# Issuing the load of the fifth weight chunk ahead of the fourth token tile's in the opening of a four-layer kernel

## The chip, the cores and the metric

The kernel runs on one core of one Trainium2 chip. The metric is the device time of one execution in microseconds (us), of which the profile's span, from the first to the last recorded instruction, is about 1.8 us less. TensorE is called PE, VectorE DVE, ScalarE ACT, GpSimd POOL; SyncE's sequencer, which issues all the loads, is SPq. Every timed run here is of the fast state, and the granted TensorE clock was 1.00 in every profile; two runs that were only looked at (e7, e8: one execution each) have no state, and only their traces are used.

## The reference, cut to what matters

Four layers over 2048 tokens of 1024 numbers (bf16), each on a layer norm and added to its input. The first and third are a linear attention, the second and fourth a gated bilinear block. Only the start of the first matters here.

```python
x = A_x
x = x + _A_ref(_layernorm(x, axis=-1), A_wqkv, A_wo)      # q, k, v = x @ wqkv; phi = exp/relu; ...
x = x + _B_ref(_layernorm(x, axis=-1), B_w_gate, B_w_up, B_w_down)
x = x + _A_ref(_layernorm(x, axis=-1), A_wqkv, A_wo)
x = x + _B_ref(_layernorm(x, axis=-1), B_w_gate, B_w_up, B_w_down)
```

## The kernel before

The tokens are cut into 16 tiles of 128 (token tile 0 is the first), the K weights into eight chunks of 128 rows (chunk 4 is the fifth). Each of these loads is 256 KB. The loads are issued from one queue in program order:

```python
    load_x(0)
    load_x(1)
    for k in range(0, 3):
        load_k(k, k + 1)
    load_x(2)
    load_k(3, 4)
    load_x(3)
    for k in range(4, 8):
        load_k(k, k + 1)
```

The first two token tiles are centred (their mean is subtracted) and turned (transposed) on PE. Then PE multiplies them by each weight chunk as it lands, two matmuls of 512 columns per tile and chunk (`k_part(t, a, b)` is tile t with chunks a to b-1). Tiles 2 and 3 are turned by DMA and follow when all eight chunks are there.

```python
            # ... tiles 0 and 1 with chunks 0 to 2, in between their transposes ...
            mean_by_halves(2, 2)
            centre_by_halves(2, 2)
            turn(XN[:, 2, :], 0, 2)            # DMA transpose of tile 2
            ln_stats(3)                        # DVE: statistics of tile 3 ...
            centre(3, stat[3][0][:, 0:1])
            turn(XN[:, 3, :], 0, 3)            # ... and its DMA transpose
            load_q()                           # the Q weights, two loads of 1 MB
            for t in range(4, NT):
                load_x(t)
            for t in range(3):
                ln_stats(t)                    # DVE: statistics of tiles 0 to 2
            for k in range(3, 6):
                for t in range(2):
                    k_part(t, k, k + 1)        # PE: chunks 3, 4, 5
            for t in range(2):
                k_part(t, 6, 8)                # PE: chunks 6 and 7 together; then phi on ACT
            k_part(2, 0, 8)
            k_part(3, 0, 8)
            # ... then the Q products of tiles 0 to 3, and so on; all that follows is unchanged
```

DVE takes its instructions in the order of the program: in the trace it begins the statistics of tile 3 at 9.54 us and those of tile 0 at 11.50. So `ln_stats(3)` stands ahead of the statistics of tile 0, which ACT's first exponential (`phi` of tile 0) needs. `phi` reads a tile's sums twice, for an exponential and for a maximum with 0. The sums stand in PSUM, the memory that PE writes, which has three places for them here; token tile 3 takes over tile 0's, and that is free only when ACT has read it.

Of the kernel before, what the change touches and what calls it, by code (L numbers as in the profile page):

```python
# [26 lines left out]
def kernel(  # L27
# [80 lines left out]
    def load(dst, src):  # L108
        nc.sync.dma_start(out=dst, in_=src)  # L109

    def load_x(t):
        load(X[:, t, :], x_view[:, t, :])

    def load_k(a, b):
        load(wkv[:, a:b, :], wqkv_v[:, a:b, D:2 * D])
# [22 lines left out]
    for k in range(0, 3):  # L138
        load_k(k, k + 1)
    load_x(2)  # L140
    load_k(3, 4)
    load_x(3)
    for k in range(4, 8):
        load_k(k, k + 1)


# [506 lines left out]
```

## Time and profile before

| | before |
|---|---|
| time, median of 3 | 1622.03 us (1621.81 to 1622.1) |
| span of the profile | 1620.1 us |
| PE busy | 99% |
| PE's waits for loads, whole kernel | one, ahead of chunk 4 |
| first matmul on chunk 4 | 10.24 us |
| first matmul of token tile 2 | 13.69 us |

The prediction below shows the lines on which this rests. One view more is needed: the issues of a narrow stretch, once around 4.0 us and once around 4.5 us. The last column is the time from issue to landing.

```profile
X<-in_A_x_dram SPq DMA_DIRECT2D x1, 256.0 KB, 5.5
...
W<-in_A_wqkv_dram SPq DMA_DIRECT2D x1, 256.0 KB, 5.7
```

Token tile 3, issued at 4.01, lands at 9.51; chunk 4, issued at 4.48, at 10.20. Both are well over 5 us under way, while the loads ahead of them land one by one: from token tile 2 on, one place in the row is 0.65 to 0.72 us. What an order of issue decides here is the order of landing. This is why exchanging two lines of the program could matter at all.

### The profile page before, as it was taken

The numbers are of one execution on the slowest core, as the hardware profiler recorded it, in microseconds if no ns is written. First come the engines' busy times: TensorE is split into PE (matmuls) and PEld (weight loads), VectorE is DVE, ScalarE is ACT, GpSimd is POOL, SyncE is SP. The second block draws the span as 40 slices with busy tenths as digits, with TensorE's granted clock in tenths as the row PEclk, the third lists the DMA queues.
The fourth block names the chain that finished last, engine by engine and source line by source line (L and its number), as shares of the span: only waits on it lengthen the run. The fifth ranks groups of instructions, "written<-read, shape, count | busy, mean of one in ns | idle before, by whom it ended". The sixth has DMA issues, their size and how long they took to land.

```text
span 1620.1 us, 18047 instructions
## 1 busy us (share of the span) xinstructions
PE 1607.5 (99%) x7710; PEld 734.5 (45%) x7861; DVE 616.6 (38%) x946; ACT 284.0 (18%) x384; POOL 54.5 (3%) x135
## 2 busy tenths in 40 slices
PE   9999999999999999999999999999999999999999
PEld 4444444444444444444444444444444444444444
DVE  6899853202311321243255798432123113211111
ACT  5522201101110110011045231011011101101110
POOL 2100000000000000010000000000000000000000
DMA  8224856512650552142420257655236306521400
GB/s 247 53 72 93 246 162 176 162 52 60 171 159 0 147 162 81 52 156 66 92 52 1 78 114 219 181 157 165 69 102 175 127 20 173 165 66 65 156 1 26
DMA packets 236719, 183.10 MB, mean 113 GB/s; under 512 B 102368, under 2 KB 217312, under 8 KB 236640
## 3 DMA queue, kind: packets, MB, share of 16 engines
q1 hardware_dynamic: 236640, 181.95, 39.0%
q8 instruction: 61, 1.00, 0.3%
q14 instruction: 18, 0.15, 0.0%
HBM read 153.09 MB, written 4.19 MB: 97 GB/s over the span
## 4 chain that ended last, share of the span: by engine, by line
PE 99%; issue 1%; DMA 0%; SPq 0%; DVE 0%
PE ps L196 50%; PE ps L538 48%; PE ps L565 1%; DMA W<-in_A_wqkv_dram 0%; PE kv L306 0%; SPq L109 0%; PE pm L328 0%; PE ps L328 0%; DVE X L546 0%
## 5 line engine op out<-in xcount | busy, mean ns | idle before, releaser
L538 PE MATMUL ps<-xT,R 128*128 128x512 bf16 x2382 | 525.9, 379 | 2.6
L538 PEld LDWEIGHTS <-R 128*128 128x128 bf16 x2432 | 238.0, 98 | 286.9
L542 DVE TENSOR_TENSOR R<-gs,ps 128x512 bf16<-128x512 f32 x224 | 153.9, 687 | 533.5 <-ACT gs L541 533.5
L196 PEld LDWEIGHTS <-R 128*128 128x128 bf16 x2248 | 220.0, 98 | 265.2
L541 ACT COPY gs<-ps 128x512 f32<-128x512 f32 x224 | 131.3, 586 | 1040.2 <-PE ps L538 1011.5
L538 PE MATMUL ps<-xT,W 128*128 128x512 bf16 x1130 | 250.4, 379 | 1.2
L196 PEld LDWEIGHTS <-xT 128*128 128x128 bf16 x1536 | 149.5, 98 | 181.4 <-issue 1.9
L196 PE MATMUL ps<-W,xT 128*128 128x512 bf16 x997 | 222.8, 379 | 1.9 <-issue 0.3
L538 PEld LDWEIGHTS <-W 128*128 128x128 bf16 x1152 | 112.7, 98 | 135.9
L196 PE MATMUL ps<-W,R 128*128 128x512 bf16 x733 | 170.1, 379 | 0.8
L546 DVE TENSOR_TENSOR X<-X,ps 128x1024 bf16<-128x1024 bf16 (+3 forms) x34 | 39.4, 1158 | 335.8 <-PE ps L196 282.8
L196 PE MATMUL ps<-R,R 128*128 128x512 bf16 x506 | 111.8, 379 | 0.4
L196 PE MATMUL ps<-PQ,R 128*128 128x512 bf16 x488 | 111.4, 379 | 0.5
L196 PE MATMUL ps<-R,xT 128*128 128x512 bf16 x502 | 110.3, 379 | 0.5
L201 ACT ACTIVATE e<-ps 128x1024 bf16<-128x1024 f32 x56 | 57.3, 1024 | 141.2 <-PE ps L196 86.0
L175 DVE BATCH_NORM_STATS2 st<-X 128x6 f32<-128x512 bf16 x128 | 81.7, 680 | 0.1
L179 POOL TENSOR_SCALAR ve<-mv 128x1 f32<-128x1 f32 x64 | 16.2, 254 | 1325.8 <-DVE mv L177 1325.8
L196 PE MATMUL ps<-GL,R 128*128 128x512 bf16 x240 | 57.8, 379 | 0.3
L196 PE MATMUL ps<-xT,R 128*128 128x512 bf16 x240 | 57.5, 379 | 0.2
L378 DVE TENSOR_TENSOR X<-X,ps 128x1024 bf16<-128x1024 bf16 x32 | 38.7, 1209 | 17.0 <-PE ps L196 17.0
L186 DVE TENSOR_SCALAR R<-X,mv,rstd 128x1024 bf16<-128x1024 bf16 x64 | 33.7, 542 | 27.3 <-POOL rstd L181 24.0
L205 DVE TENSOR_SCALAR e<-e 128x1024 bf16<-128x1024 bf16 x64 | 26.9, 421 | 38.1 <-ACT e L201 38.1
(73 smaller groups left out, 456.6 us busy)
## 6 DMA issues: line engine op xcount, KB each, us to landing
R<-in_B_w_gate_dram SPq DMA_DIRECT2D x38, 1024.0 KB, 5.4
R<-in_B_w_up_dram SPq DMA_DIRECT2D x38, 1024.0 KB, 7.6
W<-in_B_w_gate_dram SPq DMA_DIRECT2D x18, 1024.0 KB, 5.4
W<-in_B_w_up_dram SPq DMA_DIRECT2D x18, 1024.0 KB, 7.6
W<-in_A_wqkv_dram SPq DMA_DIRECT2D x10, 1024.0 KB, 6.2
W<-in_B_w_down_dram SPq DMA_DIRECT2D x6, 1024.0 KB, 11.2
X<-in_A_x_dram SPq DMA_DIRECT2D x16, 256.0 KB, 6.7
PQ<-in_B_w_down_dram SPq DMA_DIRECT2D x4, 1024.0 KB, 8.4
```

The costliest lines, as they stand in the source:

```text
L175: nc.vector.bn_stats(out=st[:, c, :], in_=X[:, t, c * NB:(c + 1) * NB])
L179: nc.gpsimd.tensor_scalar(out=ve[:], in0=mv[:, 1:2], scalar1=1e-5, scalar2=None, op0=ALU.add)
L186: nc.vector.tensor_scalar(out=dst, in0=X[:, t, :], scalar1=mv[:, 0:1], scalar2=rstd[:], op0=ALU.subtract, op1=ALU.mult)
L196: nc.tensor.matmul(out=ps[:, n, :], lhsT=lhsT, rhs=rhs[:, n * NB:(n + 1) * NB], start=start, stop=stop)
L201: nc.scalar.activation(out=e[:], in_=flat(ps), func=ACT.Exp, **sc)
L205: nc.vector.tensor_scalar(out=e[:], in0=e[:], scalar1=1.0, scalar2=EPS, op0=ALU.min, op1=ALU.add)
L378: nc.vector.tensor_tensor(out=X[:, t, :], in0=X[:, t, :], in1=flat(ps), op=ALU.add)
L538: nc.tensor.matmul(out=ps[:, n, :], lhsT=w[:, k, j * P:(j + 1) * P], rhs=xT[g % 2][:, k, :], start=(k == 0), stop=(k == KD - 1))
L541: nc.scalar.copy(out=gs[:], in_=ps[:, 0, :])
L542: nc.vector.tensor_tensor(out=hT[:, f, :], in0=gs[:], in1=ps[:, 1, :], op=ALU.mult)
L546: nc.vector.tensor_tensor(out=X[:, t, a:b], in0=X[:, t, a:b], in1=ps, op=ALU.add)
L565: nc.tensor.matmul(out=ps[:, 0, 0:b - a], lhsT=hT[:, f, tl * P:(tl + 1) * P], rhs=wd[f][:, a:b], start=(f == 0), stop=(f == KF - 1))
```

## The change

It is meant to have the chunk that PE waits for land one place earlier, at the cost of the token tile that is needed later. The whole diff:

```diff
     load_x(2)
-    load_k(3, 4)
+    for k in (3, 4):
+        load_k(k, k + 1)
     load_x(3)
-    for k in range(4, 8):
+    for k in range(5, 8):
         load_k(k, k + 1)
```

## The prediction

> **What bounds the kernel now.** I read the page first, then the chain of work that ended last, then the opening (the first 41 us) in the timeline, because the diff touches only the order of twelve loads there.
>
> The page's busy shares and the summary of the chain:
>
> ```profile
> PE 1607.5 (99%) x7710; PEld 734.5 (45%) x7861; DVE 616.6 (38%) x946; ACT 284.0 (18%) x384; POOL 54.5 (3%) x135
> ...
> PE 99%; issue 1%; DMA 0%; SPq 0%; DVE 0%
> ```
>
> TensorE (PE) is busy for 99% of 1620.1 us, and the chain is 99% PE. No other engine is above 38%. A change that adds and removes no instruction can only win time in which PE stands still. So the next question is where PE waits. The list of who waited for whom, PE's own, over the whole span, has four entries:
>
> ```profile
> PE ps L165 <- PEq L637: 0.8, 1, 0.8
> PE pt L403 <- DVE R L419: 0.7, 1, 0.7
> PE ps L196 <- issue: 0.3, 2, 0.2
> PE ps L196 <- DMA W<-in_A_wqkv_dram: 0.2, 1, 0.2
> ```
>
> Columns: total us, times, longest. The last one is the only wait for a load, and W is the tile into which the K weight chunks go. The chain of the opening says which chunk it is:
>
> ```profile
> 4.48 5.72 DMA W<-in_A_wqkv_dram
> 10.20 0.04 issue
> 10.24 2.10 PE ps L196 x9
> 12.35 0.05 issue
> 12.40 10.74 PE ps L196 x49
> ```
>
> Start, length, what. The transfer issued at 4.48 us lands at 10.20, and PE goes on at 10.24. The issues of the SyncE queue identify it:
>
> ```profile
> 3.06 0.43 SPq L109 DMA_DIRECT2D X<-in_A_x_dram  x1
> 3.53 0.43 SPq L109 DMA_DIRECT2D W<-in_A_wqkv_dram  x1
> 4.01 0.43 SPq L109 DMA_DIRECT2D X<-in_A_x_dram  x1
> 4.48 2.46 SPq L109 DMA_DIRECT2D W<-in_A_wqkv_dram  x4
> ```
>
> These are token tile 2 (the third), chunk 3 (the fourth), token tile 3 (the fourth), then chunks 4 to 7. So chunk 4, the one that the change moves, is exactly the one that PE waits for. That makes the change well aimed; what remains is how large the wait is and what comes right behind it. PE's own timeline around it:
>
> ```profile
> 6.80 3.22 PE L196 MATMUL ps<-W,xT 128*128 128x512 bf16 x14
> 10.24 10.95 PE L196 MATMUL ps<-W,xT 128*128 128x512 bf16 x49 [0.22 <-DMA W<-in_A_wqkv_dram]
> ```
>
> **What the Trainium skill says.**
> - "Perfetto Trace Analysis", section "Summary: the profiler window per engine type": a matmul's reported end is estimated, its start is observed. So I don't use the 0.22 us but starts: the last matmul of chunk 3 starts at 9.646, the first of chunk 4 at 10.241, 0.595 apart, where its neighbours are 0.216 apart. The true standstill is 0.595 - 0.216 = **0.38 us**.
> - "TensorE: Matmul & The Clock Gate", section "Back-to-back issue gap": 512 columns cost N/2.4 + 2.5, thus 215.8 ns, warm. The trace agrees (0.216, granted clock 1.00 in this stretch). The same section gives 131 ns as the sustained figure; the trace doesn't agree.
> - "DMA: Bandwidth & Descriptors", section "Queues, rings and completion order": descriptors of one queue are consumed in ring order, while completions need not be. Here they do come in order of issue, 0.6 to 0.7 us apart from token tile 2 on (below). So exchanging two issues should exchange two landings.
>
> **The change, part by part.** Nothing is added or removed: the comparison of instruction orders shows the same rows on PE, VectorE (DVE), ScalarE (ACT) and GpSimd, and on SyncE the fourth token tile and the fifth chunk have changed places. Both are 256 KB. From the trace's records of each transfer, landings before: token tile 2 8.18, chunk 3 8.84, token tile 3 9.51, chunk 4 10.20, chunk 5 10.87, chunk 6 11.53, chunk 7 12.25 us. After, by exchange: chunk 4 at 9.51, token tile 3 at 10.20, the rest unmoved.
>
> *PE's side.* Each chunk serves two token tiles with two matmuls each: 4 x 0.216 = 0.863 us. From a landing to PE's start is 0.04 us (10.199 to 10.241).
> - Chunk 4: PE is ready at 9.646 + 0.216 = 9.86, landing 9.51. No wait; start 9.86 instead of 10.24, 0.38 won.
> - Chunk 5: PE ready at 9.86 + 0.86 = 10.73, but landing + 0.04 = 10.91. A **new wait of 0.18 us**; start 10.91 instead of 11.10, 0.19 left.
> - Chunk 6: ready at 11.77, landed 11.53. No wait.
> - Chunk 7: the loop takes chunks 6 and 7 together for each token tile, so chunk 7 is wanted two matmuls later, at 11.77 + 0.43 = 12.20. Landing + 0.04 = 12.29. A **second new wait of 0.09 us**. Start 12.29 where it was 12.40.
>
> Thus the last chunk decides: its landing doesn't move, and before the change PE reached it only 0.15 us after it landed, of which 0.04 is needed anyway. The gain is 12.397 - 12.291 = **0.11 us**, of 0.38 us in sight. From 12.40 on PE runs in one piece, and the later waits are few and for its own helpers, so these 0.11 us should reach the end.
>
> *The side that pays.* Token tile 3 lands 0.69 us later. DVE starts its statistics at 9.54 today, straight after other work, 0.03 after the landing; after the change it must wait until about 10.23. Behind it in DVE's order stand the centring of tile 3 and the statistics of tiles 0 to 2, which the first exponential on ACT needs:
>
> ```profile
> ACT e L201 <- POOL rstd L181: 5.0, 1, 5.0
> ```
>
> So the whole string shifts by 0.69 us. What does PE notice?
> - Transpose of tile 3 lands at 14.76, later 15.45; its matmuls begin at about 17.04. Slack 1.6.
> - PSUM: the matmuls of tile 3 wait for ACT to have read tile 0's sums. ACT ends that at 16.14, later 16.83; wanted at 17.04 (12.29 + 6 x 0.216 + 16 x 0.216). **Slack 0.2**, 0.15 with a semaphore.
> - Q weights, issued behind the transposes: second half lands at 21.23, later 21.92; wanted at about 22.21. **Slack 0.29**.
> So both stay just hidden. Nothing to subtract.
>
> Sum: 1622.03 - 0.11 = 1621.9 us.
>
> **The rivals.**
> 1. *The whole wait goes*: 0.38 us, thus 1621.65. For it: chunk 4's wait is the only one that the views show. Against: the landings of chunks 5 and 7 are 0.24 and 0.15 us ahead of PE today and come by the same full queue. It would need all of them to come earlier, and the change gives them nothing.
> 2. *The late token tile makes a new stall*: if tile 3 slips by 0.9 us or more rather than 0.69, ACT frees PSUM too late or the Q weights come too late, and PE loses 0.1 to 0.5 us; the time would be 1622.0 to 1622.4. For it: slacks of only 0.2 to 0.3. Against: equal sizes, evenly spaced landings.
> 3. *Nothing to be seen*: the three runs of before differ by 0.29 us (1621.81 to 1622.1), more than the gain. If landings wander by 0.1 us between executions, the gain is between nought and 0.2 and drowns. This is what I expect of the end-to-end times, with the trace showing the steps.
>
> A loss or gain of 2% would be 32 us. All of PE's waits in the opening together are 1.7 us, so neither is within reach.
>
> **Range and chances.** Centre 1621.9. Downwards, rival 1 plus the scatter of before gives 1621.4; upwards, rival 2 gives 1622.4; 0.1 us more on each side for another day's scatter. Within 2%: 0.99.
>
> **What would show it.** In the changed kernel's profile: (a) chunk 4 lands near 9.5 and token tile 3 near 10.2; (b) PE's one wait for W, 0.22 us long by the view, gives way to two smaller ones, before chunk 5 (0.18 by starts, so hardly visible in the view because the modelled matmul ends cover 0.16 of any wait) and before chunk 7 (0.09, invisible there); (c) the matmul that first uses chunk 7 starts at about 12.29 instead of 12.40; (d) DVE idles about 0.65 us before the statistics of tile 3, and ACT's first exponential begins at about 14.7 instead of 14.02; (e) no new PE wait at 17.0 or 22.2. It would be wrong if landings do not follow the order of issue, if chunk 7 lands at another time than 12.25, or if (e) fails.

## The result, and the profile after

| | before | changed |
|---|---|---|
| median of 6 runs | 1622.07 us | 1621.88 us |
| lowest to highest | 1621.67 to 1622.96 | 1621.26 to 1622.7 |
| span of the profile | 1620.1 us | 1620.2 us |

The ratio is 0.9999, with a 95% interval from 0.9986 to 1.0011: the same. (A ratio is the mean time of one kernel's runs over that of the other's of the same rounds, so not quite the ratio of the medians.)

The span of the changed kernel is even 0.11 us longer, though its time is shorter. That asks for the trace. First a trap: the page of the changed kernel says

```profile
PE 1616.5 (100%) x7861; PEld 734.9 (45%) x7861; DVE 616.7 (38%) x946; ACT 283.8 (18%) x384; POOL 54.3 (3%) x135
```

PE seems 9 us busier than before. It isn't: before, the trace held 7710 matmul records for 7861 weight loads, so 151 were missing. For that reason the starts below are taken from the weight loads, one to each matmul and complete in both. (While PE runs without a gap, the weight load for the next matmul starts within 0.01 us of the matmul before it.)

The issues at 4.01 and 4.49 us of the changed kernel, in the same view as above:

```profile
W<-in_A_wqkv_dram SPq DMA_DIRECT2D x1, 256.0 KB, 5.7
...
X<-in_A_x_dram SPq DMA_DIRECT2D x1, 256.0 KB, 5.8
```

The two have changed places: chunk 4 landed at 9.68 (before 10.20), token tile 3 at 10.33 (before 9.51). The chain of the opening, changed kernel:

```profile
4.96 6.05 DMA W<-in_A_wqkv_dram
11.01 0.04 issue
11.06 11.97 PE ps L197 x54
```

The chain no longer ends at the transfer issued at 4.48 but at the next, issued at 4.96: chunk 5. PE now waits for that one. And it waits again behind it, which this view doesn't show. The timeline of the weight loads does, first before, then changed; of the idle time in brackets 0.12 us stands between any two loads:

```profile
8.57 1.18 PEld L196 LDWEIGHTS <-xT 128*128 128x128 bf16 x6
10.24 3.77 PEld L196 LDWEIGHTS <-xT 128*128 128x128 bf16 x18 [0.50 <-issue]
...
9.04 1.60 PEld L197 LDWEIGHTS <-xT 128*128 128x128 bf16 x8 [0.35 <-issue]
11.06 1.17 PEld L197 LDWEIGHTS <-xT 128*128 128x128 bf16 x6 [0.42 <-issue]
12.51 1.39 PEld L197 LDWEIGHTS <-xT 128*128 128x128 bf16 x7 [0.28 <-issue]
```

So PE waited 0.38 us ahead of chunk 4 before, and 0.30 us ahead of chunk 5 and 0.16 us ahead of chunk 7 in the changed kernel; in this execution also 0.24 us ahead of chunk 3, which the change leaves alone. The first matmul of token tile 2 began at 13.80, 0.11 later than before, and every later instruction of PE kept this offset to the end (1617.26 for the last weight load, against 1617.15). So the whole difference of the two spans was made in the first 14 us. But chunk 7 landed at 12.47 in this trace and at 12.25 in the other, though the loads ahead of it are the same eleven. Is that the change's doing, or does it wander?

DVE paid as expected. Its line for the statistics of tile 3, in DVE's timeline:

```profile
10.36 1.29 DVE L176 BATCH_NORM_STATS2 st<-X 128x6 f32<-128x512 bf16 x2 [1.26 <-DMA X<-in_A_x_dram]
```

In brackets stands the idle time before it and what ended it: the landing of the late token tile. Before, it began at 9.54 straight after other work. ACT's first exponential followed at 14.84 instead of 14.02. PE noticed nothing of it: ACT had read tile 0's sums at 16.96, and PE wanted their place at 17.25.

### The profile page after: what moved, and what is told of

Its sections match the earlier page's. It is cut to its first block, busy times and chain, and to the rows that moved or that the text cites. A ratio compares the mean times of both kernels' runs of the same rounds, so it can differ in the third digit from the quotient of the medians.

```text
span 1620.2 us, 18198 instructions
## 1 busy us (share of the span) xinstructions
PE 1616.5 (100%) x7861; PEld 734.9 (45%) x7861; DVE 616.7 (38%) x946; ACT 283.8 (18%) x384; POOL 54.3 (3%) x135
## 4 chain that ended last, share of the span: by engine, by line
PE 99%; DMA 0%; SPq 0%; issue 0%; DVE 0%
PE ps L197 50%; PE ps L539 48%; PE ps L566 1%; DMA W<-in_A_wqkv_dram 0%; PE kv L307 0%; SPq L109 0%; PE pm L329 0%; PE ps L329 0%; DVE X L547 0%
```

## The experiments

The theory: in the changed kernel the landing of the last chunks sets when PE gets to token tile 2, in the kernel before that of chunk 4, and these two are worth almost the same. The rivals: the change costs a fixed 0.1 us; the late token tile does not matter; or it does, and costs as much as was won.

### e1 and e2: both kernels once more

No edit. Five timed runs and one more trace of each.

> The kernel before, unchanged, against itself: how far times and landings wander. Theory (the landing of the last weight chunk sets the start of token tile 2 in the changed kernel, and almost does so before): landings move by up to 0.2 us from one execution to the next, PE waits only ahead of chunk 4 (0.3 to 0.5 us by starts), and the start of token tile 2's K matmuls follows the landing of chunk 4, about 3.5 us after it. Rival (landings are steady, and the 0.1 us by which the changed kernel's profiled run came out longer is a cost of the change): landings within 0.05 us of 10.20 for chunk 4 and 12.25 for chunk 7. Ratio of times 1.000 either way, scatter of the single runs some 0.5 us.

> The changed kernel, unchanged, once more. Theory: PE waits ahead of chunk 5 and chunk 7, and token tile 2's K matmuls start 1.34 us after the landing of chunk 7 (0.04 and six matmuls of 0.216 us), whatever that landing is; 13.6 us if it is 12.25, 13.8 if it is 12.47. Rival (the change costs a fixed 0.1 us): token tile 2 starts at 13.8 again although chunk 7 lands at 12.25. Ratio of times within 0.0005 of 1.

Times: before 1621.94 us (median of 5) against 1621.76 of the nine runs of the same kernel beside it, ratio 1.0 (0.9987 to 1.0012); changed 1621.99, ratio 1.0001 (0.9988 to 1.0013). So the times can't tell 0.1 us: the same kernel differs from itself by 0.18 in the median. In the trace of e1 PE waited 0.23 us ahead of chunk 4, less than the 0.3 to 0.5 expected, and 0.16 ahead of chunk 1, which was not expected.

The traces can. PE's timeline of the changed kernel:

```profile
6.66 5.21 PE L197 MATMUL ps<-W,xT 128*128 128x512 bf16 x23
12.05 9.23 PE L197 MATMUL ps<-W,xT 128*128 128x512 bf16 x42 [0.18 <-DMA W<-in_A_wqkv_dram]
```

Here PE's wait for a load has moved from chunk 4 to chunk 7, which landed at 12.01. (The view says 0.18 because a matmul record is missing; by starts it is 0.13, after 0.05 ahead of chunk 5.) The chain of the same trace jumps from that landing straight to token tile 2 and beyond:

```profile
6.16 5.86 DMA W<-in_A_wqkv_dram
12.01 0.04 issue
12.05 10.74 PE ps L197 x49
```

The start of token tile 2 in all traces of the two kernels, a third look at the changed one (e8, below) included:

| trace | chunk 4 lands | chunk 5 | chunk 7 | token tile 2 starts |
|---|---|---|---|---|
| before, first | 10.20 | 10.87 | 12.25 | 13.69 |
| before, e1 | 10.28 | 10.95 | 12.30 | 13.78 |
| changed, first | 9.68 | 11.01 | 12.47 | 13.80 |
| changed, e2 | 9.25 | 10.59 | 12.01 | 13.35 |
| changed, e8 | 9.88 | 11.24 | 12.50 | 13.87 |

Before: 3.49 and 3.50 us after chunk 4. Changed: 1.34 and 1.34 us after chunk 7, and in e8 2.63 us after chunk 5. These are the prediction's steps: 0.04 us and sixteen, six or twelve matmuls of 0.216. The fixed cost falls: the start of token tile 2 follows the landings of its own trace (13.35 with chunk 7 at 12.01, where that rival asked for 13.8 again), and the working below leaves nothing over for it. Landings wander by up to 0.65 us in the changed kernel alone (chunk 5), where the rival of e1 asked for 0.05; e1 alone, off by 0.08 and 0.05, would hardly have decided that.

To take the luck out, I ran the prediction's own recursion (PE takes a chunk when it is done with the one before it or 0.042 us after its landing, whichever is later; 0.2158 us a matmul) on each trace's landings and its start of chunk 3, once in either order, chunk 4 taking the eighth or ninth place of landing:

| trace | tile 2 measured | order before | order changed | difference |
|---|---|---|---|---|
| before, first | 13.694 | 13.694 | 13.586 | 0.11 |
| before, e1 | 13.775 | 13.777 | 13.639 | 0.14 |
| changed, first | 13.802 | 13.826 | 13.803 | 0.02 |
| changed, e2 | 13.347 | 13.393 | 13.349 | 0.04 |
| changed, e8 | 13.868 | 14.052 | 13.869 | 0.18 |

For the kernel that ran, it meets the measured start within 0.002 us each time. The other column is an estimate, since one execution has one order only. By it the change is worth 0.02 to 0.18 us, 0.10 in the mean.

One thing came unlooked for. In e2 the 0.35 us by which the opening was ahead of the first trace of before held until 972 us and were gone after it. PE's timeline there shows sixteen small matmuls (32*32, each with its own `tile_position` in the program), of which these two lines hold four:

```profile
971.93 0.39 PE L329 MATMUL ps<-PQ,KVb 32*32 32x512 bf16 x2
972.29 0.39 PE L329 MATMUL pm<-PQ,KVb 32*32 32x512 bf16 x2
```

In the traces without this gap all sixteen start within 0.05 us; here the ninth starts 0.36 us after the eighth, and it waits for no semaphore. e8 and e10 come back to it.

### e3 and e4: token tile 3 later still

e3 loads it after all the chunks, e4 after chunk 5.

```diff
     load_x(2)
-    load_k(3, 4)
+    for k in range(3, 8):        # e4: range(3, 6)
+        load_k(k, k + 1)
     load_x(3)
-    for k in range(4, 8):        # e4: range(6, 8)
-        load_k(k, k + 1)
```

> Token tile 3 is loaded after all eight chunks, so that chunk 7 lands a whole place earlier (about 11.55) and token tile 3 at about 12.25. Theory: PE's waits for chunks vanish and token tile 2 starts at about 13.3 (0.38 earlier than before), but the statistics of tile 3 stand ahead of those of tile 0 on DVE, so ACT's first exponential slips by 2.7 us to about 16.8, ACT frees tile 0's sums at about 18.9, and PE stands still some 2.1 us before token tile 3's matmuls: the kernel is 1.8 us slower than before (1.3 to 2.2), ratio 1.0011. Rival (the landing of token tile 3 has slack and does not matter): no stall, 0.4 us faster.

> Token tile 3 one place later still than in the changed kernel, behind chunk 5; it lands at about 10.9 to 11.0. Theory: PE waits only ahead of chunk 7 (0.25 us), token tile 2 starts 1.34 us after that landing as in the changed kernel, so nothing more is won; but ACT frees tile 0's sums 1.36 us later than before, at 17.5, where PE wants them at 17.0: a stall of about 0.5 us before token tile 3, the kernel 0.4 us slower than before (0.2 to 0.7). Rival (the slack of 0.2 us was reckoned too small): no stall, 0.1 us faster than before.

e3: 1623.54 us against 1621.76 before, 1.78 more; ratio 1.0013 (1.0001 to 1.0026; one of its five runs, 1625.63, lies apart from the other four, 1623.26 to 1623.94). PE's waits in e3:

```profile
PE ps L195 <- ACT R L201: 1.7, 1, 1.7
PE ps L164 <- PEq L636: 0.8, 1, 0.8
```

From chunk 3 on, PE ran through all chunks without a wait and began token tile 2 at 13.21. Ready for tile 3 at 13.21 + 16 x 0.2158 = 16.66, it started only at 18.57: 1.91 us, where 2.1 was forecast. The chain gives the string of causes:

```profile
15.80 0.58 POOL rstd L180
16.38 0.02 issue
16.40 0.02 ACT e L200
16.43 0.99 issue
17.41 1.12 ACT R L201
18.53 0.04 issue
18.57 5.99 PE ps L195 x27
```

POOL's factor for tile 0 comes late since DVE first does tile 3; then ACT reads tile 0's sums twice, and at 18.53 their place in PSUM is free. e4: 1622.10 us, 0.34 more than before, ratio 1.0002 (0.9988 to 1.0015), so by the times alone the same. In its trace PE was ready for tile 3 at 17.05 and started at 17.55, a stall of 0.50 as forecast; ahead of chunk 7 it waited 0.07 where 0.25 was expected. PE's line:

```profile
17.55 6.64 PE L197 MATMUL ps<-W,xT 128*128 128x512 bf16 x29 [0.33 <-ACT R L203]
```

So the landing of token tile 3 has slack for the one place that the change takes, and not enough for a second. The rival of "doesn't matter" falls, and so does that of a loss already at one place: the three traces of the changed kernel show no wait before tile 3.

### e5: chunk 7 wanted later

On top of the change:

```diff
-            for k in range(3, 6):
+            for k in range(3, 8):
                 for t in range(2):
                     k_part(t, k, k + 1)
-            for t in range(2):
-                k_part(t, 6, 8)
```

> The changed kernel, but the loop takes chunk 6 for both token tiles before chunk 7, so chunk 7 is wanted 0.43 us later. Theory: the wait ahead of chunk 7 vanishes; only chunk 5's remains, and token tile 2's K matmuls start 2.63 us (0.04 and twelve matmuls of 0.216) after chunk 5's landing, 0.09 to 0.16 us earlier than the changed kernel would with the same landings. Rival (chunk 7's landing decides whatever the order of use): token tile 2 starts 1.34 us after chunk 7's landing, or later. Too small for the times: ratio within 0.0005 of 1.

Chunk 5 landed at 10.87, token tile 2 started at 13.50: 2.63 us later, as forecast. Chunk 7 landed at 12.28, so its tie of 1.34 us would have given 13.62. The wait ahead of chunk 7 is thus due to the order of use, and the one ahead of chunk 5 (0.08 us) remains. Time 1621.73 against 1621.83, ratio 0.9999 (0.9987 to 1.0012): too small to tell.

### e6 and e9: everything in time

Token tile 3 behind chunk 5 as in e4, chunk 7 apart as in e5, and:

```diff
+            load(wq[:, 0:1, :], wqkv_v[:, 0:1, 0:D])     # ahead of tile 3's transpose
+            ln_stats(0)
             ln_stats(3)
             centre(3, stat[3][0][:, 0:1])
             turn(XN[:, 3, :], 0, 3)
-            load_q()
+            for a, b in ((1, 4), (4, 6), (6, 8)):
+                load(wq[:, a:b, :], wqkv_v[:, a:b, 0:D])
             # ...
-            for t in range(3):
+            for t in range(1, 3):
                 ln_stats(t)
```

> Everything at once: token tile 3 behind chunk 5, chunk 7 apart, the statistics of tile 0 ahead of those of tile 3 on DVE, and 256 KB of the Q weights issued ahead of tile 3's transpose. Theory: after chunk 3 PE runs through without a wait for a chunk, for PSUM, for the transpose or for Q; token tile 2 starts 4.32 us after chunk 3's first matmul and the Q part 6.9 us after that, some 0.3 us earlier than in the kernel before with the same landings; time 0.3 us under before, at the edge of what the runs resolve. Rival (other waits come up in the place of those removed): a wait of over 0.1 us before token tile 3 or in the first Q product, and no gain.

> The sixth run's kernel once more, because its five timed runs (mean 1621.82 us) stood against nine of before (mean 1621.85) and showed no gain, while its trace showed PE without any wait after chunk 3. Theory: PE again runs through from chunk 3 to Q without a wait; the start of the whole stretch moves with the landing of chunk 0 and of the first token tile by up to 0.5 us between executions, so that the 0.3 to 0.4 us won drown in the times: mean of before less mean of this between 0 and 0.6 us. Rival (the gain is lost later, for good): the trace shows a wait later on that takes back 0.3 us or more.

In e6 the waits of PE over the whole kernel are these:

```profile
PE ps L166 <- PEq L639: 0.8, 1, 0.8
PE ps L197 <- issue: 0.3, 2, 0.2
```

No load, no ACT, no transpose; by starts, too, there is no gap from chunk 3 to the Q products. From the first matmul on chunk 0 to the first of token tile 2 it took 7.39 us in e6, 7.39 in e9; before 7.77 and 7.90; in the changed kernel 8.15, 7.68 and 7.81. So the opening is indeed shorter by 0.4 to 0.5 us than before. Yet the ten timed runs of e6 and e9 have a mean of 1621.94 us, and all 38 timed runs of the kernel before a mean of 1621.91: no gain. The forecasts of the times failed: e6 was to be 0.3 us under before and its mean was 0.04 under; e9 was to be 0 to 0.6 under and was 0.06 over. Three terms are seen. In e9 the last part of the Q weights came late and PE waited 0.07 us for it (0.23 in e10). The stretch from the last weight load of the kernel to the end of the span was 3.06 to 3.09 us in e6, e9 and e10, against 2.90 to 2.93 in all the other traces: 0.14 to 0.19 us more. The traces' semaphore records tell where: at the end SyncE checks one semaphore pair after another, about 0.06 us each. These kernels issue 282 transfers, the others 280 (the Q weights come in four parts, not two), and the last store is now told by the pair that stands second in this row, not fifth, so that three more checks follow it: SyncE's wait for it ends 0.98 to 0.99 us before the end of the span, against 0.79 before. That is read from the traces; no run tests it. And the start wanders: chunk 0 landed at 5.41 in e6, at 6.38 in e9, issued at 1.64 us in both behind the same two loads. The first matmul on it began at 5.58 and 6.42, and the gapless opening passed that on in full: token tile 2 began at 12.97 and 13.81. So this version beats neither kernel by its times.

### e7: token tile 3 last, statistics of tile 0 first

```diff
     # loads as in e3
+            ln_stats(0)
             ln_stats(3)
             # ...
-            for t in range(3):
+            for t in range(1, 3):
                 ln_stats(t)
```

> Token tile 3 last as in the third run, but with the statistics of tile 0 ahead of those of tile 3 on DVE, so that ACT and PSUM no longer depend on the late tile. Theory: the wait for ACT (1.2 us in the third run) goes, but tile 3's transpose still lands at about 17.1, a wait of 0.7 to 0.9 us there, and then the second half of the Q weights, issued behind that transpose, lands at 23.5 where it is wanted at 22.3: 1.2 us of new wait. In all only 0.1 to 0.3 us better than the third run, still 1.1 to 1.7 us over before. Rival (the wait for ACT is the whole cost): as fast as before or 0.3 us faster.

PE's timeline (single look):

```profile
17.47 3.63 PE L195 MATMUL ps<-W,xT 128*128 128x512 bf16 x16 [0.66 <-DMA xT<-R]
21.34 1.89 PE L195 MATMUL ps<-W,xT 128*128 128x512 bf16 x8 [0.24 <-DMA W<-in_A_wqkv_dram]
23.95 0.38 PE L195 MATMUL ps<-W,xT 128*128 128x512 bf16 x1 [0.73 <-DMA W<-in_A_wqkv_dram]
```

The wait for ACT is gone, and three others have come in its place: by starts, 0.84 us for the transpose of tile 3, 0.41 for the first half of the Q weights (not forecast), 0.88 for the second. In all 2.13 us, more than the 1.91 of e3, where I had expected 0.1 to 0.3 less (and 1623.79 us in its one execution, against e3's 1623.54). So ACT was not the whole cost. The two sums come from different landings, though: token tile 3 landed 0.95 us before PE began token tile 2 in e7, but 1.32 before it in e3. An estimate that takes these 0.37 us off gives 1.76 for e7, 0.15 less than e3, as forecast; which of the two holds, one trace each can't tell. A late token tile is thus tied to PE by three strings, over ACT, the transpose and the Q weights. The first and the last are almost equally long: in e3, with 1.91 us already lost to ACT, the second half of the Q weights landed only 0.20 us before PE wanted it. Cutting one string wins little.

### e8 and e10: the gap at 972 us

e8 is the changed kernel a third time. e10 is e9 with the next layer's gate and up weights issued later:

```diff
-        load_gu(0)
-        load_gu(1)
-        load_gu(2)
-        for j in DN_ORDER[:2]:
-            load_dn(j)
         o = [out_unit(t) for t in range(NT)]
-        do([o[0]] + d(12) + o[1:3] + d(13) + o[3:5] + d(14) + o[5:7] + d(15))
+        do([o[0]] + d(12))
+        load_gu(0)
+        load_gu(1)
+        do(o[1:3] + d(13))
+        load_gu(2)
+        do(o[3:5] + d(14) + o[5:7] + d(15))
+        for j in DN_ORDER[:2]:
+            load_dn(j)
```

> A third look at the changed kernel. In the second look 0.34 us won in the opening were lost at 972 us, where the ninth of sixteen small matmuls, which waits for no semaphore, started 0.36 us late. Theory: that was a thing of one execution; here the offset of PE's instructions against the kernel before stays what it is at token tile 2 up to the end, except for such single events, and token tile 2 starts 1.34 us after chunk 7's landing. Rival: a stage in the middle always takes back what the opening wins, so the same place shows it again whenever the opening is ahead of the kernel before.

> As the ninth run, and the gate, up and down weights of the next layer are issued after the transpose of the twelfth token tile's quotient and later, not before it. In three of ten traces PE started the ninth of sixteen small matmuls at 972 us late by 0.09 to 0.36 us; in those three the instruction fetch (16 KB, a queue of its own) that precedes it ended under 1.2 us ahead of that matmul, in the seven others 1.5 us or more ahead. Theory (that fetch shares the DMA engines with the gate and up weights and comes late for it): without them in flight it ends over 2 us ahead of the matmul, and no gap. Rival (the fetch's time is set by PE's own place in the program): it ends 1 to 2.5 us ahead as before. Time as the ninth run's within 0.5 us, if the later weights are still in time for their layer.

e8 kept its offset from 14 us to the end and has no gap. Its other forecast, token tile 2 at 1.34 us after chunk 7, missed by 0.03 us, as chunk 5 decided there. Over all twelve traces the gap came in three: 0.36 us in e2, 0.30 in e7, 0.09 in e5, always before the same ninth matmul. e7 was behind the kernel before by 1.6 us at that place and had it; e6 was ahead by 0.7 and hadn't. So the rival that a middle stage takes back whatever the opening wins falls. In the three traces the 16 KB instruction fetch before it ended 1.06, 1.17 and 1.18 us ahead of that place, in the nine others 1.39 to 2.52 us ahead. That fits a fetch that comes late, but my reason for its lateness failed: in e10, with the gate and up weights out of the way, it ended 1.39 us ahead, not over 2. e10 had no gap. Its time was 1621.92 against 1621.93, ratio 1.0 (0.9988 to 1.0013). The cause of the gap stays open.

## Why the prediction was right

*Chunk 4's wait goes.* Shown: in none of the changed kernel's three traces did PE wait for it.

*Two new waits, chunk 5 and chunk 7.* Shown in kind, the one for chunk 7 in two traces of three. In size the forecast of 0.18 and 0.09 us met 0.30 and 0.16, 0.05 and 0.13, 0.10 and none: the terms follow from the landings of each execution, which I had taken as fixed at those of one trace. This is the weakest step: "the rest unmoved" holds for their order, not for their times, which moved by up to 0.65 us. So one of the prediction's own signs failed: chunk 7 was to land at 12.25 and its first matmul to start at 12.29 instead of 12.40, and they came at 12.47 and 12.51, 12.01 and 12.05, 12.50 and 12.57. In the first trace of the changed kernel PE thus reached token tile 2 at 13.80, 0.11 us later than in the first of before, not 0.11 earlier.

*The last chunk decides, 0.11 us won of 0.38.* Shown, with chunk 5 deciding in one trace of three. With equal landings the exchange is worth 0.10 us in the mean of five traces, by the recursion; this is an estimate, for no execution has both orders. The times neither confirm nor refute it: over all timed runs the means are 1621.91 us (38 runs, standard deviation 0.33) and, changed, 1621.93 (11 runs, 0.38). The median of 1621.88 lies at the forecast 1621.9, but its closeness is luck at this scatter. That the offset of the opening reaches the end held in two of the three traces of the changed kernel; in e2 the gap at 972 us took 0.36 us of it.

*The side that pays stays hidden.* Shown: at one place of lateness PE has no new wait before token tile 3 or in the Q products; at two places e4 loses 0.50 us where 0.5 was reckoned, and at four places e3 loses 1.91. The reckoned slack of 0.2 us was 0.29 in the first trace of the changed kernel. The prediction speaks of the statistics of tiles 0 to 2 as what the first exponential needs; it needs tile 0's. And it left out one string, the transpose of token tile 2: that landed 0.52, 0.50 and 0.34 us before PE began that tile, so it cost nothing.

*DVE's idle time.* The forecast 0.65 us was 1.26 and 0.76 in two traces, since token tile 2 landed early there; what counted, ACT's first exponential, was forecast at 14.7 and came at 14.84, 14.41 and 15.07.

*The rivals.* The whole wait did not go: chunk 5 or 7 took its place. The late tile made no stall. The third, that nothing would be seen in the times, is what happened.

## What to carry to other kernels

When loads land one behind the other from a full queue, moving the one that is waited for lets the next become the bound; the gain is at most the smallest lead that any later load of the row still has, so work out the lead of each, not the wait of one. Ask the same of the load that was moved back: how many strings tie it to the busy engine, and how much slack each has. And a gain below the scatter of the runs is to be judged in traces by what follows what, with the landings of the same trace, never by comparing one trace with another.

## What the Trainium skill lacked or had wrong

- "TensorE: Matmul & The Clock Gate", section "Back-to-back issue gap", has about 131 ns a matmul as sustained rate for 512 columns in a stream of weight load and matmul pairs. Here such a stream ran at 0.216 us a matmul, as from 12.40 us on in the chain of the kernel before (49 in 10.74 us, the last of them reported with 0.379), which is the section's other formula, given there for isolated matmuls.
- "Perfetto Trace Analysis", section "Summary: the profiler window per engine type", says that a matmul's end is estimated, not how much this hides. Here a matmul is reported with 0.379 us at a spacing of 0.216, so idle time is understated by 0.16 us each time: 0.22 shown for 0.38 before, and nothing for 0.16 ahead of chunk 7 in the changed kernel.
- "DMA: Bandwidth & Descriptors", section "Specifications", lists a limit of about 358 GB/s per core from HBM and doesn't say there that a core alone can exceed it; a note in the same page's section "Measured (HBM→SBUF, 128 partitions, SWDGE, issued from GpSimd)" gives this figure to two cores that stream together. For this kernel on one core, 256 KB landed every 0.65 to 0.72 us in the first trace of before, from token tile 2 on; 262,144 bytes in 0.67 us are 391 GB/s, which agrees with the note.
- No page that I read gives how far the landing of a load at the start of a program wanders: chunk 0, issued at 1.64 or 1.65 us in every trace behind the same two loads, landed between 5.20 and 6.40 us.
- Nor does one give a gap as that in the group of sixteen small matmuls, before one that waits for no semaphore: 0.09 to 0.36 us in three of twelve traces.
